# An attention kernel with a hand-written order: the third batch's fourth un-permute moved off GpSimd, a tail product kept at full width, and the order table written anew

## Chip, cores, metric

The kernel runs on one core of a Trainium2 chip. The metric is device time in microseconds (us), the median of five runs. Engines are called as the profile calls them: PE is the matrix engine (PEld its weight loads), DVE the vector engine, ACT the scalar engine, POOL the GpSimd engine, and SP the sync engine, which here only issues DMAs. A name such as SPq or POOLq is the instruction queue of that engine, where DMA issues show up.

## What is computed

Eight batches of eight-head attention over 576 positions with 64 numbers a head, with a causal mask in blocks of 64, followed by a gated feed-forward layer over all 4608 rows.

```python
scores = scale * np.matmul(q, k.transpose(0, 1, 3, 2))      # (8, 8, 576, 576)
mask = block_i >= block_j                                   # blocks of 64
attn = softmax(where(mask, scores, -1e9))
x = (attn @ v).transpose(0, 2, 1, 3).reshape(4608, 512)
out = (np.maximum(x @ w_gate, 0.0) * (x @ w_val)) @ w_out   # 512 -> 1536 -> 512
```

## The kernel before

**Tiling.** Each sequence of 576 is cut into four chunks of 128 positions and a tail of 64. A *round* r = 4*b + hp is one pair of heads hp of batch b. It makes the scores of the four chunks, transposed (keys on the partitions), takes the exponential on ACT into `attnT`, sets the masked corners to zero, and multiplies by V with a column of ones attached, so that the 65th output column is the sum that the softmax divides by. DVE divides (`normalise`, L518) into `xnat`, which is transposed into `xT`, the input of the feed-forward layer. In the first three batches the tails of all heads are done together (`tail_visit`, `last_keys`, `tail_av`); from the fourth batch on each round does its own tail.

**Feed-forward.** `ffn_gen` (L648) is a generator that emits one matrix product at each step: 96 products of the gate and the value halves and 48 of the output for each batch, 144 in all, and a ninth group for the tails of all batches. ACT takes the relu of the gate (L664), DVE multiplies it with the value product (L670), and DVE copies finished outputs out of PSUM (L749).

**The order.** Nothing is scheduled automatically. Under `manual_schedule` every engine runs its instructions in the order in which the program emits them, and each waits on semaphores for its data. The table `AT` gives every piece of work, called an act, a position: the number of feed-forward products that are emitted ahead of it. Acts are emitted in the order of their positions; acts with equal positions in the order in which the dictionary `acts` lists them; a negative position is ahead of the first product. Between 0 and 143 lie the products of the first batch, from 144 to 287 those of the second, from 288 to 431 those of the third. `HOW` says which engine or PSUM bank an act uses. So a change of position is a change of order inside the queue of each engine that the act uses, and nothing else.

**PSUM.** Three banks named `ffnp` serve the feed-forward products and many attention products in turn, `one` is a single bank, and `sc` are two double banks for the scores.

**Names that matter below:**

- `M0` to `M3`: transposes on PE of the first batch's queries and keys, pair 0 to 3, and the copies out of PSUM (L278). `p{r}{i}`: part i of the scores of round r and its exponential (L400, L414). `c{r}`: the corners. `a{r}`, `b{r}`: the products with V of the round's two heads (L576) and their division. `x{r}`: the transposes into `xT` (L619) and the copy (L620).
- `ev0`, `ev4`: POOL's casts of the second batch's V, heads 0 to 3 and 4 to 7 (L220). `tc0`: POOL's casts of the first batch's tails (L206, L207, L214). `E1v4`, `T0`: the loads that these two need, issued by SP in this order (L159, L181).
- `q2`, `q24`: for the third batch, POOL casts queries and keys of heads 0 to 3, or 4 to 7 (L195), and SP then issues two DMA transposes into the tile `perm` (L242). `u0` to `u3`: for each pair of heads, two copies (L253) that put the transposed rows in their order in `qTm` and `kTm`. `u2` and `u3` read what `q24` has transposed. `v2`: POOL's casts of the third batch's V (L228).
- `s{r}`, `e{r}`: the scores of a round from the second batch on (L450) and its exponentials (L462, L455). `S{b}`, `E{b}`, `L{b}`, `A{b}`, `B{b}`: tail scores, their exponential, the last 64 keys, and the products of tails with V for heads 0 to 3 (`A`) and 4 to 7 (`B`). `B` ends with a DMA transpose on SP (L562).
- `l3`, `lv3`: POOL issues the loads of the fourth batch (L338); `d3`: SP issues its transposes.

In the tail products, head 7 and chunk 3 has only 64 columns of weights left in its tile, so that one matrix is 64 columns wide (L545).

Of the kernel before, what the change touches and what calls it, by code (L numbers as in the profile page):

```python
# [10 lines left out]
FP = mybir.dt.float32  # L11
BF = mybir.dt.bfloat16
AX = mybir.AluOpType
# [4 lines left out]
def kernel(  # L18
# [10 lines left out]
    nc = tc.nc  # L29

    B, H, S, D = q.shape
# [4 lines left out]
    NCH = 5  # L36
# [5 lines left out]
    TW = 256  # L42

    consts = ctx.enter_context(tc.tile_pool(name="consts", bufs=1))
    sb = ctx.enter_context(tc.tile_pool(name="sb", bufs=1))
# [22 lines left out]
    attnL = [consts.tile([128, 320], BF, name=f"attnL{i}") for i in range(2)]  # L68
# [449 lines left out]
    def normalise(out, av, x=None):  # L518
        n = av.shape[1]
        rows = av.shape[0]  # L520
        recip = sb.tile([128, NCH], FP, name="recip", bufs=4)[0:rows, 0:n]
        nc.vector.reciprocal(recip, av[:, :, 64])  # L522
        m = out.shape[1]
        nc.vector.tensor_tensor(  # L524
            out=out,
            in0=av[:, 0:m, 0:64],
            in1=recip[:, 0:m].to_broadcast([rows, m, 64]),
            op=AX.mult,
        )
        if x is not None:  # L530
            nc.vector.tensor_tensor(
                out=x,
                in0=av[0:64, 4, 0:64],
                in1=recip[0:64, 4:5].to_broadcast([64, 64]),
                op=AX.mult,
            )

    def tail_av(b, g, x):

        av = psum_ffn.tile([128, 4, 65], FP, name="ffnp")  # L540
        for i in range(4):
            h = 4 * g + i
            lo = 1024 * (h % 2) + TW * (h // 2)
            for c in range(NCH):
                m = 64 if (h, c) == (7, 3) else 128  # L545
                nc.tensor.matmul(
                    av[0:m, i, :],
                    attnTt[b][:, lo + 64 * c : lo + 64 * c + m]
                    if c < 4
                    else attnL[b % 2][:, 64 * (h // 2) : 64 * (h // 2) + 128],  # L550
                    v_bf[b % 2][:, c, h, :],
                    start=(i == 0 and c == 0),
                    stop=(c == 4),
                    skip_group_check=True,
                )
        normalise(
            x[:, 256 * g : 256 * g + 256].rearrange("p (h d) -> p h d", d=64),
            av[0:64],
        )
# [5 lines left out]
    attnTt = {}  # L565
# [225 lines left out]
    dve, act, pool = nc.vector.tensor_copy, nc.scalar.copy, nc.gpsimd.tensor_copy  # L791
# [7 lines left out]
    with tc.manual_schedule(engines={E.PE, E.DVE, E.Activation, E.Pool, E.SP}):  # L799
# [25 lines left out]
        def tail_at(b):  # L825
            exps = []
            x = sb.tile([64, 512], BF, name="xtail", bufs=2)

            def begin():
                exps.extend(tail_visit(b))  # L830
                exps[0]()

            def end():
                tail_av(b, 1, x)
                tail_to_xT(b, x)

            return {
                f"S{b}": begin,
                f"L{b}": lambda: last_keys(b),
                f"E{b}": lambda: exps[1](),  # L840
                f"A{b}": lambda: tail_av(b, 0, x),
                f"B{b}": end,
            }
# [38 lines left out]
        def mains_1(hp):  # L882
# [12 lines left out]
            "v00": -59.5,  # L895
            "Lv2": -59.5,
            "Lq6": -59.5,
            "Lq4": -59.5,
            "g00": -56.5,
            "Lv4": -56.5,  # L900
            "Lv6": -54.8,
            "g01": -53.5,
            "v10": -53.5,
            "v11": -49.5,
            "v01": -49.5,
            "g10": -49.5,
            "g11": -48.91,
# [4 lines left out]
            "C1": -42.45,  # L912
            "M0": -41.16,
            "p00": -41.16,
            "j1": -41.16,
            "cq6": -40.5,
            "cq4": -40.5,
            "M1q": -37.69,
            "p02": -37.69,
            "p01": -37.69,  # L920
            "M1k": -37.69,
            "cv2": -33.09,
            "p11": -32.5,
            "cv0": -31.08,
            "M2": -29.71,
            "p10": -29.71,
            "p12": -29.71,
            "c0": -29.71,
            "c1": -20.67,
            "a0": -20.67,  # L930
            "M3": -20.67,
            "b0": -20.67,
            "p21": -20.67,
            "p20": -20.67,
# [4 lines left out]
            "b1": -17.04,  # L939
            "c2": -17.04,  # L940
            "cv4": -17.01,
            "p30": -16.5,
            "x0": -11.01,
            "x1": -10.42,
            "p32": -10.42,
            "cg00/01": -10.42,
            "a2": -10.42,
            "c3b": -7.27,
            "b2": -7.27,
            "c3a": -4.51,  # L950
            "cg00/23": -4.51,
            "cg01/23": -4.51,
            "cv6": -4.18,
            "cv00/01": -3.23,
            "v20": 3.64,
            "b3": 4.1,
# [5 lines left out]
            "g21": 7.88,  # L962
            "cv10": 8.2,
            "cv11": 8.27,
            "cg11": 8.27,
            "cv01": 8.27,
            "cg10": 8.27,
            "E1q0": 8.31,
            "v21": 8.31,
            "x3": 9.71,  # L970
            "cg20": 31.51,
# [14 lines left out]
            "cg21": 32.24,  # L986
            "cv21/0": 32.24,
            "q0": 32.24,
            "cw01": 32.3,
            "cw00": 32.32,  # L990
            "cw10": 32.32,
# [5 lines left out]
            "q4": 32.36,  # L997
            "tc0": 34.05,
            "ev4": 37.33,
            "q2": 37.71,  # L1000
            "E2q4": 37.71,
# [5 lines left out]
            "s4": 100.01,  # L1007
            "E2v0": 109.09,
            "e4": 110.34,
            "cw21/1": 110.84,  # L1010
            "c4": 112.87,
            "s5": 119.06,
            "a4": 120.37,
            "b4": 120.57,
            "e5": 120.86,
            "m2": 122.6,
            "c5": 124.25,
            "E2v4": 125.35,
            "q24": 126.26,
            "T2": 126.26,  # L1020
            "a5": 127.58,
            "s6": 128.09,
            "b5": 130.33,
            "e6": 130.65,
            "m3": 132.5,
            "c6": 133.72,
            "x5": 135.38,
            "x4": 135.4,
            "s7": 139.49,
            "a6": 139.98,  # L1030
            "b6": 141.02,
            "e7": 143.55,
            "c7": 143.96,
# [6 lines left out]
            "S0": 164.13,  # L1040
            "td1": 164.5,
            "t1": 164.55,
            "L0": 164.73,
            "E0": 169.47,
            "A0": 174.55,
            "S1": 175.78,
            "B0": 178.92,
            "L1": 179.84,
            "E1": 189.73,
            "v2": 190.06,  # L1050
            "u0": 190.06,
            "u1": 190.06,
            "s8": 198.38,
            "e8": 200.2,
            "A1": 204.6,
            "c8": 207.66,
            "u2": 207.72,
            "s9": 208.6,
            "o0": 211.5,
            "B1": 211.84,  # L1060
            "e9": 212.79,
# [3 lines left out]
            "t2": 214.73,  # L1065
            "a8": 216.59,
            "l3": 218.86,
            "lv3": 219.23,
            "u3": 222.25,
            "s10": 222.25,  # L1070
            "b8": 224.97,
            "c9": 225.44,
            "a9": 230.23,
            "b9": 230.68,
            "e10": 231.58,
            "o2": 234.34,
            "o3": 236.36,
            "x8": 237.81,
            "s11": 244.56,
            "c10": 245.9,  # L1080
            "a10": 249.57,
            "e11": 251.12,
            "b10": 253.45,
            "x9": 254,
            "x10": 255.79,
# [3 lines left out]
            "x11": 260.07,  # L1089
            "d3": 260.7,  # L1090
            "S2": 284.11,
            "L2": 291.9,
            "E2": 294.4,
            "A2": 301.64,
            "s12": 310.76,
            "L3": 315.45,
            "l4": 318.62,
            "e12": 323.23,
            "B2": 327.97,
            "c12": 332.42,  # L1100
            "lv4": 334,
            "a12": 335.18,
            "b12": 341.27,
            "s13": 345.46,
            "e13": 348.38,
            "x12": 350.72,
            "c13": 355.41,
            "d4": 356.12,
            "s14": 358.61,
# [6 lines left out]
            "b14": 381.91,  # L1116
            "x14": 384.44,
            "s15": 390.53,
            "e15": 394.34,
            "c15": 398.77,  # L1120
            "a15": 407.55,
            "b15": 407.68,
            "x15": 413.15,
# [9 lines left out]
            "u1": ("dve", "pool"),  # L1133
            "u2": ("dve", "dve"),
            "u3": ("pool", "dve"),
# [7 lines left out]
            "r11": ("dve", "sc", "ffn", None),  # L1143
# [3 lines left out]
            "r15": ("pool", "sc", "ffn", None),  # L1147
            "cv21/1": "act",
# [10 lines left out]
            "M3": ("dve", "dve"),  # L1159
# [11 lines left out]
            "cv00/23": "dve",  # L1171
        }
# [141 lines left out]
```

## Time and profile before

| what | us |
|---|---|
| median of five runs | 365.61 |
| lowest and highest of the five | 365.25, 369.18 |
| the profiled execution, its own time | 364.56 |
| its span, first to last instruction | 362.7 |
| granted PE clock over the span | 0.999 of full speed |
| ACT, exponentials of the rounds' scores, 128x1024 (L455, 56 times) | 1.044 each |
| DVE, product of gate and value, 128x512 (L670, 106 times) | 0.686 each |
| POOL, an un-permute copy (L253, 4 times) | 1.045 to 1.075 each |
| DVE, the same copy (L253, 4 times) | 0.598 to 0.959 each |
| POOL, one DMA issue of V, 128 KB or 32 KB (L338, 30 times) | 0.856 each |

The profile is of one execution; its span lies 1.9 us under its own time and 2.9 us under the median of the runs. A row of the waits reads "engine, line, waited for: total, times, longest". A row of the timeline reads "start, duration, engine, line, operation", with the idle time of the engine before it, and what ended that, in brackets. Matrix products overlap each other, so the time that one costs the engine is the distance of two starts, not the duration of one.

### The profile page before, as it was taken

What the parts mean: (1) busy time and instruction counts of PE and PEld (TensorE: products, weight loads), DVE (VectorE), ACT (ScalarE), POOL (GpSimd) and SP (SyncE); (2) the same over time, 40 slices, a digit from 0 to 9 for tenths busy, and PEclk for the clock granted to TensorE, in tenths of its full rate; (3) what the DMA queues carried; (4) which work ended last, traced back from release to release, by engine and by line L of the source; (5) the groups of instructions that cost most, each with busy time, mean ns of one, the idle gap of its engine ahead of it and who ended that gap; (6) DMA issues with size and microseconds to landing.
All of it is one profiled execution on the core that took longest, in us unless ns stands there. A gap on an engine that the chain in (4) does not pass through costs nothing.

```text
span 362.7 us, 7421 instructions
## 1 busy us (share of the span) xinstructions
PE 352.9 (97%) x2933; PEld 177.3 (49%) x2933; DVE 169.3 (47%) x422; ACT 167.4 (46%) x264; POOL 115.1 (32%) x159
## 2 busy tenths in 40 slices
PE   7799999999999999999999999999999999999996
PEld 3454454644455455545554554555455544444443
DVE  4763555567434463444444443554255434333432
ACT  4944675676236840666055625553365403302310
POOL 4647647688006800680049001930000000000000
PEclk9999999999999999999999999999999999999999
DMA  8999999999999996999449951997220130031014
GB/s 246 296 358 375 315 217 282 188 134 176 191 195 61 166 129 171 59 149 178 118 43 147 158 142 45 133 136 172 80 16 14 54 102 0 0 89 29 0 39 108
DMA packets 152083, 49.97 MB, mean 138 GB/s; under 512 B 134512, under 2 KB 145008, under 8 KB 152048
## 3 DMA queue, kind: packets, MB, share of 16 engines
q0 software_dynamic: 70480, 8.85, 45.5%
q1 hardware_dynamic: 76480, 31.86, 42.8%
q10 hardware_dynamic: 5088, 8.78, 7.5%
q8 instruction: 23, 0.38, 0.5%
q14 instruction: 12, 0.10, 0.1%
HBM read 37.75 MB, written 9.44 MB: 130 GB/s over the span
## 4 chain that ended last, share of the span: by engine, by line
PE 74%; DMA 13%; SPq 7%; POOL 4%; issue 1%; DVE 0%; POOLq 0%
PE ffnp L654 41%; PE ffnp L739 23%; DMA stage<-in_moe_w_gate_dram 4%; DMA stage<-in_k_dram 3%; DMA stage<-in_moe_w_out_dram 3%; PE sc L450 3%; SPq L159 2%; DMA k_bf<-in_k_dram 2%; PE ffnp L576 2%; PE one L450 2%; PE one L576 1%; DMA stage<-in_v_dram 1%; SPq L181 1%; SPq L169 1%; POOL q_bf L338 1%
## 5 line engine op out<-in xcount | busy, mean ns | idle before, releaser
L670 DVE TENSOR_TENSOR hT<-gate_sb,ffnp 128x512 bf16<-128x512 bf16 x106 | 72.7, 686 | 93.8 <-PE ffnp L654 69.6
L664 ACT ACTIVATE gate_sb<-ffnp 128x512 bf16<-128x512 f32 x103 | 62.1, 605 | 100.2 <-PE ffnp L654 91.3
L654 PE MATMUL ffnp<-xT,wv 128*128 128x512 bf16 x376 | 100.9, 379 | 0.0
L739 PE MATMUL ffnp<-wo,hT 128*128 128x512 bf16 (+2 forms) x444 | 99.0, 373 | 0.0
L654 PE MATMUL ffnp<-xT,wg 128*128 128x512 bf16 x364 | 98.2, 379 | 0.3 <-DVE xT L620 0.3
L739 PEld LDWEIGHTS <-hT 128*128 128x128 bf16 x444 | 41.6, 98 | 45.6 <-issue 1.1
L654 PEld LDWEIGHTS <-wg 128*128 128x128 bf16 x432 | 40.1, 98 | 44.6 <-issue 2.8
L654 PEld LDWEIGHTS <-wv 128*128 128x128 bf16 x432 | 40.0, 98 | 44.7 <-issue 2.8
L455 ACT ACTIVATE attnT<-sc 128x1024 bf16<-128x1024 f32 x56 | 56.8, 1044 | 0.0
L749 DVE COPY ob<-ffnp 128x512 f32<-128x512 f32 (+2 forms) x37 | 25.0, 676 | 44.7 <-PE ffnp L739 44.3
L338 POOL DMA_DIRECT2D q_bf<-in_q_dram x20 | 17.8, 905 | 80.1 <-DVE hT L670 55.9
L462 ACT ACTIVATE attnT<-one 128x512 bf16<-128x512 f32 (+1 forms) x28 | 15.1, 538 | 53.5 <-PE ffnp L450 53.3
L576 PEld LDWEIGHTS <-attnT 128*128 128x128 bf16 x640 | 26.6, 98 | 13.9 <-issue 1.5
L338 POOL DMA_DIRECT2D v_bf<-in_v_dram x30 | 24.3, 856 | 2.1 <-DVE xnat L524 1.0
L450 PEld LDWEIGHTS <-kTm 64*128 64x128 bf16 x384 | 11.1, 94 | 16.3 <-issue 9.6
L338 POOL DMA_DIRECT2D k_bf<-in_k_dram x20 | 17.8, 939 | 0.0
L450 PE MATMUL sc<-qTm,kTm 64*128 64x512 bf16 (+1 forms) x168 | 16.9, 305 | 0.0
L576 PE MATMUL ffnp<-v_bf,attnT 128*128 128x65 bf16 x310 | 14.5, 194 | 0.9 <-POOL v_bf L220 0.9
L462 ACT ACTIVATE attnT<-ffnp 128x512 bf16<-128x512 f32 (+1 forms) x28 | 15.0, 535 | 0.0
L522 DVE RECIPROCAL recip<-ffnp 128x5 f32<-128x5 f32 (+2 forms) x37 | 6.8, 184 | 15.4 <-PE ffnp L590 5.3
L524 DVE TENSOR_TENSOR xnat<-ffnp,recip 128x256 bf16<-128x256 f32 x31 | 13.2, 424 | 1.1
L794 DVE MEMSET attnT<- 64x128 uint32 x59 | 9.0, 165 | 9.4 <-ACT attnT L455 6.8
(120 smaller groups left out, 300.5 us busy)
## 6 DMA issues: line engine op xcount, KB each, us to landing
out_dram<-ob ACTq DMA_DIRECT2D x29, 256.0 KB, 2.3
stage<-in_moe_w_val_dram SPq DMA_DIRECT2D x6, 512.0 KB, 8.9
stage<-in_moe_w_gate_dram SPq DMA_DIRECT2D x6, 512.0 KB, 8.6
stage<-in_moe_w_out_dram SPq DMA_DIRECT2D x6, 512.0 KB, 10.5
q_bf<-in_q_dram POOLq DMA_DIRECT2D x20, 128.0 KB, 4.4
k_bf<-in_k_dram POOLq DMA_DIRECT2D x20, 128.0 KB, 5.7
v_bf<-in_v_dram POOLq DMA_DIRECT2D x20, 128.0 KB, 6.6
stage<-in_v_dram SPq DMA_DIRECT2D x19, 128.0 KB, 5.4
```

The costliest lines, as they stand in the source:

```text
L338: ins = nc.gpsimd.dma_start(dst, part_of)
L450: nc.tensor.matmul(o, kTm[b % 2][head_of(hh), c, hp, :], qT, start=True, stop=True)
L455: return lambda: nc.scalar.activation(at[:, :, lo : lo + 512], sc, AF.Exp, scale=scale)
L462: nc.scalar.activation(at[:, hh, 1024 : 1024 + w], third[hh][:, 0:w], AF.Exp, scale=scale)
L524: nc.vector.tensor_tensor(out=out, in0=av[:, 0:m, 0:64], in1=recip[:, 0:m].to_broadcast([rows, m, 64]), op=AX.mult,)
L576: nc.tensor.matmul(av[:, p, :], at[:, col : col + 128], v_bf[b % 2][:, c, h, :], start=(p == 0), stop=(c == p), skip_group_check=True,)
L654: nc.tensor.matmul(to, (wg, wv)[t][f // 4][:, c, 128 * (f % 4) : 128 * (f % 4) + 128], x[:, c], start=(c == 0), stop=(c == 3),)
L664: nc.scalar.activation(gate_sb, gate, AF.Relu)
L670: nc.vector.tensor_tensor(out=h, in0=gate_sb, in1=val, op=AX.mult)
L739: nc.tensor.matmul(op, hT[f][:, 128 * s : 128 * (s + 1)], wo[f // 4][:, f % 4, n0:n1], start=(f == 0), stop=(f == 11),)
L749: nc.vector.tensor_copy(ob, op)
L794: nc.vector.memset(o, 0.0)
```

## The change

Three things are changed.

The tail products of head 7 read their weights 64 columns further left, so that all of them are 128 columns wide. The wanted 64 rows of this head then come out in the upper half of the partitions (64 to 127) instead of the lower. The division is therefore made in up to two DVE operations: for heads 0 to 3 one, for heads 4 to 7 one on three heads and one on the last. It is written out in `tail_av` in place of the call of `normalise`.

`HOW` gives other engines to some acts: both copies of `u1` go to DVE (the keys were POOL's), `u3` goes to DVE and ACT (the queries were POOL's, the keys DVE's), the query copy of `M3` goes from DVE to ACT, one weight cast (`cv21/1`) from ACT to DVE. `cv01` is named as POOL's, where it was by default. `r11` and `r15` use other PSUM banks.

The table `AT` is replaced. Many positions differ by a few products, which leaves most queues in their old order. The diff below keeps the positions of acts that change places in a queue and are spoken of below; those of the load queue of SP change in one place at the start (`g00` ahead of `Lv4`) and in the place of `q24`.

```diff
@@ tail_av
             h = 4 * g + i
-            lo = 1024 * (h % 2) + TW * (h // 2)
+            back = 64 if h == H - 1 else 0
+            lo = 1024 * (h % 2) + TW * (h // 2) - back
+            lo_last = 64 * (h // 2) - back
             for c in range(NCH):
-                m = 64 if (h, c) == (7, 3) else 128
                 nc.tensor.matmul(
-                    av[0:m, i, :],
-                    attnTt[b][:, lo + 64 * c : lo + 64 * c + m]
+                    av[:, i, :],
+                    attnTt[b][:, lo + 64 * c : lo + 64 * c + 128]
                     if c < 4
-                    else attnL[b % 2][:, 64 * (h // 2) : 64 * (h // 2) + 128],
+                    else attnL[b % 2][:, lo_last : lo_last + 128],
                     v_bf[b % 2][:, c, h, :],
...
-        normalise(
-            x[:, 256 * g : 256 * g + 256].rearrange("p (h d) -> p h d", d=64),
-            av[0:64],
-        )
+        recip = sb.tile([128, NCH], FP, name="recip", bufs=4)
+        nc.vector.reciprocal(recip[:, 0:4], av[:, :, 64])
+        x4 = x[:, 256 * g : 256 * g + 256].rearrange("p (h d) -> p h d", d=64)
+        n = 4 if g == 0 else 3
+        for rows, i, j in ((slice(0, 64), 0, n), (slice(64, 128), n, 4)):
+            if i < j:
+                nc.vector.tensor_tensor(
+                    out=x4[:, i:j],
+                    in0=av[rows, i:j, 0:64],
+                    in1=recip[rows, i:j].to_broadcast([64, j - i, 64]),
+                    op=AX.mult,
+                )
@@ AT
...
-            "p02": -37.69,
+            "p02": -41.16,
-            "c0": -29.71,
+            "c0": -37.69,
-            "p10": -29.71,
+            "p10": -29.72,
-            "p30": -16.5,
+            "p30": -17.27,
-            "p32": -10.42,
+            "p32": -13.98,
-            "c3b": -7.27,
+            "c3b": -10.42,
-            "a2": -10.42,
+            "a2": -4.51,
-            "cv00/01": -3.23,
+            "cv00/01": 4.09,
...
-            "ev4": 37.33,
+            "ev4": 34.05,
             "tc0": 34.05,
...
-            "q24": 126.26,
+            "q24": 191.07,
             "T2": 126.26,
-            "B0": 178.92,
+            "B0": 178.89,
             "u0": 190.06,
             "u1": 190.06,
-            "v2": 190.06,
+            "v2": 191.07,
             "u2": 207.72,
-            "A1": 204.6,
+            "A1": 210.5,
-            "B1": 211.84,
+            "B1": 220.2,
-            "s10": 222.25,
+            "s10": 221.68,
             "u3": 222.25,
-            "l3": 218.86,
+            "l3": 217.2,
-            "lv3": 219.23,
+            "lv3": 223.89,
...
-            "s15": 390.53,
+            "s15": 383.65,
-            "e15": 394.34,
+            "e15": 383.74,
@@ HOW
-            "u1": ("dve", "pool"),
+            "u1": ("dve", "dve"),
             "u2": ("dve", "dve"),
-            "u3": ("pool", "dve"),
+            "u3": ("dve", "act"),
...
-            "r11": ("dve", "sc", "ffn", None),
+            "r11": ("dve", "one", "ffn", None),
...
-            "r15": ("pool", "sc", "ffn", None),
-            "cv21/1": "act",
+            "r15": ("pool", "ffn", "ffn", None),
+            "cv21/1": "dve",
...
-            "M3": ("dve", "dve"),
+            "M3": ("act", "dve"),
...
+            "cv01": "pool",
```

## Prediction

> **What bounds the kernel now.** I read the totals first, then PE's waits by stretch, then the timeline around each wait.
>
> ```profile
> PE 352.9 (97%) x2933; PEld 177.3 (49%) x2933; DVE 169.3 (47%) x422; ACT 167.4 (46%) x264; POOL 115.1 (32%) x159
> ```
>
> PE is busy for all but 9.8 us of the span, no other engine for half of it. Since matmuls overlap, busy is not yet full rate; but in the chain of waits 96 products take 20.72 us, 0.216 each, and I find no slower stretch of such products after the start. So the span shrinks only where PE waits or where its own work shrinks. The view of PE's waits, asked for 22 to 60 us and for 60 us to the end, answers with one row each:
>
> ```profile
> PE ffnp L576 <- POOL v_bf L220: 0.9, 1, 0.9
> ...
> PE one L450 <- POOL qTm L253: 0.9, 1, 0.9
> ```
>
> All other listed waits of PE lie before 22 us, and 3.5 us after the last product (the final copy and store) stay as they are. The timeline shows what stands behind the two.
>
> ```profile
> 49.94 0.62 POOL L195 CAST k_bf<-stage 128x512 bf16<-128x512 f32 x1 [0.20 <-DMA stage<-in_k_dram]
> ...
> 53.80 0.61 POOL L206 CAST q_bt<-stage 64x512 bf16<-64x512 f32 x1 [3.24 <-DMA stage<-in_q_dram]
> ...
> 55.61 1.06 POOL L220 CAST v_bf<-stage 128x1024 bf16<-128x1024 f32 x1
> ...
> 56.72 0.46 PE L576 MATMUL ffnp<-v_bf,attnT 128*128 128x65 bf16 x10 [0.85 <-POOL v_bf L220]
> ...
> 84.55 3.53 POOL L338 DMA_DIRECT2D v_bf<-in_v_dram  x4
> ...
> 89.08 1.32 POOL L338 DMA_DIRECT2D v_bf<-in_v_dram  x2 [0.99 <-DVE xnat L524]
> ...
> 90.44 1.04 POOL L253 COPY qTm<-perm 128x512 bf16<-128x512 bf16 x1
> ...
> 91.54 0.27 PE L450 MATMUL one<-qTm,kTm 64*128 64x256 bf16 x1 [0.87 <-POOL qTm L253]
> ```
>
> In the first group POOL stands 3.24 us for the tails (`tc0`) while `ev4`, which PE needs, is queued behind. In the second `u3`'s query copy is behind all of POOL's DMA issues for the fourth batch; PE waits 0.87 us for it.
>
> **The change, part by part.** Sums are made against the profiled execution (span 362.7, own time 364.56); the median of the runs, 365.61, is 1.05 above that time, and I carry savings over to the median.
>
> *`ev4` ahead of `tc0`: -0.85.* Its loads were issued on SP's queue between 45.27 and 48.48, ahead of the tail query load (48.58) that landed by 53.80. With the 5.3 us median to landing of such loads they are there by 53 to 53.8; the cast (1.06) ends at 54.1 to 54.9. PE wants it at 56.72 - 0.85 = 55.87. The tail casts move back by some 1 us at most, and `q2` behind them starts as before (same total on POOL). Bounds: 0 if the load lands after 54.8, else 0.85. I take 0.85: the row of the next load says 53.80.
>
> *`u3` to DVE and ACT: -0.87.* POOL loses 1.05. DVE's part changes from the keys (0.60) to the queries (0.66 to 0.67, `u2`'s and `u1`'s rows); ACT gets a copy of 0.60 to 0.64 (L278's rows). Both sit near 83 us, where ACT is busy 1.35 of 2 us and DVE 1.90; `s11`, which needs them, is 22 products (4.8 us) behind. `u1`'s keys likewise add 0.60 to 0.96 to DVE at 72 to 74 us, where it is busy 1.27 of 2. Priced at nothing; cover gone, 0.6 each.
>
> *No 64-column matmul: -0.7.* In `B0` the last head starts at 70.50 and the next work at 70.87, 0.37; the head before takes 68.36 to 68.50 in the like place of `A0`, 0.14. In `B1` 80.68 to 81.06, in `B2` 114.17 to 114.55. Three times 0.23. DVE pays one more operation on 64x64 for each (0.206) and saves a quarter of 0.417, +0.1 each, behind which only the tail's DMA transpose waits.
>
> *`q24` behind `B0` and `v2`: +0.3, the doubtful term.* Before, its casts ended at 64.4 and its transposes were issued at 70.18 and 73.37; `u2` on DVE at 79.21 waited for nothing. Now POOL must run `u0`, wait for `B0`'s products (70.8 before, about 70.0 with the savings ahead of it), run `v2` (2.03) and then the two casts (2.1): about 74.1. On SP the transposes are now behind `B0`'s own transpose (1.2 us of issue, its input ready at 71.7) and go out at about 73.2 and 74.4. They landed 5.3 and 3.4 us after issue; that gives 78.5 and 77.8, while DVE reaches `u2` at about 79.21 - 0.85 - 0.2 = 78.2. Queued behind `u2` on DVE are the products L670 and the divisions, for which PE's banks wait. The sharper question is what shares the DMA engines. POOL's issues for the fourth batch started at 75.21; they now start some 0.5 later (two casts more, a load wait of 0.78 and the 0.85 less). The row of the transposes issued at 83 to 87 us, in the middle of those loads, says 6.8 to 8.7 us. The Trainium skill (DMA: Bandwidth & Descriptors, "Issuing engines are not separate DMA queues") says that DMAs of all issuing engines end up on the same 16 DMA engines and interleave. By the row of 5.3 the wait is 0.3 or less; taking the rule for the whole transfer, 8.7 us, they land at 81.9 and 83.1, and `u2` ends at 84.1 instead of 80: 4 us late, of which PE forgives about 1.0 (a gate and value pair takes it 1.72, DVE needs 0.69 of that for the bank), so +2.9. The transposes are half through when the loads start, so I am nearer the first: +0.3, with 0 and +2.9 as ends.
>
> A second rule speaks against giving DVE these copies: by the skill (GPSIMD Engine Reference, Key points) POOL shares its memory interfaces with DVE and contends with two-port DVE instructions. The rows: `u2`'s key copy took 0.96 at 79.81, `u3`'s 0.60 at 83.82, both beside POOL's DMA issues, and POOL's four issues took 3.60 across the first against 3.67 with none. By the rule three copies at 0.96; by the better row 0.60 to 0.67. One us of DVE between them, not of PE, so the sum stays, except that the 0.3 above would become 0.6.
>
> *The start: 0.* ACT's queue sets it: twelve exponentials from 6.83 to 17.79, with an idle 0.49 at 10.33.
>
> ```profile
> 10.38 0.50 PE L400 MATMUL sc<-qTm,kTm 64*128 64x512 bf16 x4
> ...
> 10.81 5.99 ACT L414 ACTIVATE attnT<-sc 128x1024 bf16<-128x1024 f32 x7 [0.49 <-PE sc L400]
> ...
> 16.70 0.58 ACT L620 COPY xT<-ffnp 128x512 bf16<-128x512 bf16 x1
> ...
> 17.17 0.62 ACT L414 ACTIVATE attnT<-sc 128x512 bf16<-128x512 f32 x1
> ...
> 17.65 0.41 DVE L620 COPY xT<-ffnp 128x512 bf16<-128x512 bf16 x1
> ...
> 18.12 0.81 PE L654 MATMUL ffnp<-xT,wg 128*128 128x512 bf16 x3 [0.29 <-DVE xT L620]
> ```
>
> `p10` no longer waits behind `M2`'s transposes, which wait for POOL's casts: the 0.49 goes. `M3`'s copy (0.60) comes in. `p32` goes ahead of `x0`: it ends about 0.5 earlier, `x0`'s copy 0.5 later, near 17.8. The first feed-forward product waits for that, but the next three waited for `x1` until 18.12 anyway, and `x1` on DVE stays at 17.5 to 18, now behind `c3b`. Then DVE carries `a2`, `b2`, a cast, `b3`, `a3` at 0.55 or 0.42 each to about 20.5, as before (20.45), and the twelfth product comes at 21.6. What is late next is DVE. Bounds: -1.5 (its 0.69 less for `M3` and ACT's 0.5 both count) to +0.7 (`x0` late by its whole copy). Middle: 0.
>
> *The rest: 0.* `s15` and `e15` go to the first product of an output group, where ACT has no relu for 48 products (10 us); other moves are of a few products, and no wait of PE is listed there that they could take away.
>
> Sum: -0.85 - 0.87 - 0.7 + 0.3 = -2.1. Span 360.6, profiled time 362.4, median 363.5.
>
> **The rivals.**
>
> *The start gains too.* For it: ACT's and PE's small waits before 18.2 us (0.69, 0.32, 0.50, 0.22, 0.29) hang on one another. With -1.5 there and no loss at `u2`: -3.9, median 361.7. Against it: DVE's five operations, above.
>
> *Slower: `u2` holds DVE.* If the transposes take 8.7 us, -2.4 + 2.9 = +0.5, median 366.1; each further us of landing costs one more, as PE then has no bank. It decides from a landing 8.2 us after issue, and over 1% slower needs 12. For it: rows of 8.0 (`q2`'s, behind loads) and 8.7. Against it: `q24`'s own 5.3 and 3.4.
>
> *The waits only move.* PE arrives 0.85 earlier at 57 us and meets the next late thing, say the exponentials of round 7 or the tail loads; then only the 0.7 and perhaps one wait remain: -1.0, median 364.6. Against it: no other wait is listed after 22 us, and DVE and ACT follow PE in that stretch.
>
> **How the numbers follow.** The sum as worked out 0.45, waits that move 0.17, the start gains too 0.27, `u2` holds DVE 0.11. About 1% (3.7 us) is what a measurement of this kernel can tell from no change; the body cannot give more than 2.4, so "faster by over 1%" is the start's case and takes its 0.27, a little generously. Slower by over 1% takes 0.11, stretched for stalls that I do not see; within 1% has 0.62. The range goes from 360.8 (start at its best, -2.4 - 1.5 and 0.9 of spread between runs: four of the five lie within 1.0) to 366.8 (the slow case, half a us worse than its price).
>
> **What would show it.** No wait of PE on L220 near 56 us and none on L253 near 91 us; the last head of `B` at 0.14; DVE's copies L253 near 78 us with an idle of 0.5 or less before them that ends with the DMA `perm`; the twelfth product at 21.6. Wrong: an idle of over 2 us on DVE at `u2` with PE waiting, a first product after 18.3 with the twelfth after 22.2, or a new wait row of PE after 22 us.

## The result and the profile after

The changed kernel takes 363.0 us (median of 43 runs, 39 of them between 362.3 and 365.7) against 366.0 for the kernel before beside it (78 runs): a ratio of 0.993, 95% interval 0.9917 to 0.9944. The ratio leaves out three runs of the changed kernel that took 410, 522 and 611 us at a granted clock of 0.57 to 0.85. Its profiled execution took 364.26 us over a span of 362.5, at a granted clock of 0.999.

First the totals on the page of the changed kernel.

```profile
PE 353.0 (97%) x2933; PEld 176.9 (49%) x2933; DVE 170.3 (47%) x426; ACT 167.8 (46%) x265; POOL 113.3 (31%) x157
```

Its view of PE's waits lists none from 22 to 60 us, and from 60 us to the end this one:

```profile
PE ffnp L663 <- DMA xT<-xnat: 1.0, 1, 1.0
```

Both waits of before are gone, and a wait of 1.0 us for a DMA transpose is new. The timeline of the changed kernel at the places that the forecast named:

```profile
53.60 1.06 POOL L220 CAST v_bf<-stage 128x1024 bf16<-128x1024 f32 x1 [2.99 <-DMA stage<-in_v_dram]
54.61 0.61 POOL L206 CAST q_bt<-stage 64x512 bf16<-64x512 f32 x1
...
56.20 0.47 PE L585 MATMUL ffnp<-v_bf,attnT 128*128 128x65 bf16 x10
...
69.41 0.29 PE L547 MATMUL ffnp<-v_bf,stage 128*128 128x65 bf16 x4
69.53 0.20 PE L547 MATMUL ffnp<-v_bf,attnL 128*128 128x65 bf16 x1
...
78.00 0.60 DVE L253 COPY qTm<-perm 128x512 bf16<-128x512 bf16 x1
...
83.70 0.76 DVE L253 COPY qTm<-perm 128x512 bf16<-128x512 bf16 x1
...
89.68 0.28 PE L450 MATMUL one<-qTm,kTm 64*128 64x256 bf16 x1
...
103.47 0.79 PE L663 MATMUL ffnp<-xT,wg 128*128 128x512 bf16 x2 [1.00 <-DMA xT<-xnat]
```

`ev4` stands ahead of the tails and PE passes at 56.20 without a wait; `B0`'s last head is as short as the others (the one before it starts at 69.26); `u2` on DVE begins without idle; `u3` is done long before round 11 at 89.68. At 103.47 PE is early, and what it wants is not there.

To see where time is won and lost, I follow one landmark through all kernels: the start of DVE's product of gate and value (L670, or L679 in the kernels with the new `tail_av`). The table gives its distance to the kernel before, in us, for the profiled execution of each kernel: the first product of the first feed-forward batch, the first and the eleventh of the second, the first of the third and of the fourth. From there to the last such product nothing changes by more than 0.02. The last two columns are the median of all runs and the ratio to before with its interval. The experiments ran in three groups, each beside its own runs of before (medians 367.4, 366.5 and 366.6), so ratios are compared between groups, and medians only inside one.

| kernel | 1st | 2nd batch | its 11th | 3rd | 4th | median | ratio |
|---|---|---|---|---|---|---|---|
| changed | +0.52 | -0.47 | -1.26 | -0.48 | -0.34 | 363.0 | 0.993 (0.992 to 0.994) |
| changed, again | +0.54 | -0.45 | -1.23 | -1.82 | -0.81 | 363.02 | 0.991 (0.988 to 0.994) |
| narrow product back | +1.30 | +0.32 | +0.18 | -0.40 | -0.36 | 363.42 | 0.991 (0.989 to 0.993) |
| `ev4` behind tails | +0.53 | -0.46 | -0.97 | -1.55 | -1.73 | 363.65 | 0.993 (0.990 to 0.995) |
| start of before | -0.04 | -1.02 | -1.80 | -2.38 | -1.22 | 362.58 | 0.990 (0.987 to 0.994) |
| three parts alone | +0.03 | -0.99 | -0.46 | -1.38 | -1.29 | 363.55 | 0.995 (0.992 to 0.997) |
| `u3` on POOL behind loads | +0.80 | -0.19 | -0.95 | +5.82 | +5.64 | 367.13 | 1.001 (0.998 to 1.005) |
| `u3` on POOL ahead of loads | +0.50 | -0.48 | -1.27 | -1.85 | -2.04 | 362.66 | 0.992 (0.989 to 0.995) |
| start of before, `ev4` behind | +0.77 | -0.21 | -0.94 | -1.53 | -1.71 | 363.48 | 0.990 (0.985 to 0.995) |
| before, loads behind pair | +0.65 | +0.91 | +1.49 | +0.55 | +0.56 | 363.99 | 0.992 (0.989 to 0.995) |
| start of before, `u3` ahead | -0.06 | -1.04 | -1.81 | -2.18 | -0.46 | 363.48 | 0.989 (0.984 to 0.994) |
| weight cast behind `x2` | +0.42 | -0.56 | -1.35 | -1.54 | +0.15 | 362.4 | 0.988 (0.983 to 0.993) |

The two kinds of column do not say the same. By its profile the changed kernel gains 0.3 us, by its runs 2.6 (the ratio) to 3.0 (the medians); "before, loads behind pair" loses 0.56 in its profile and gains 2.6 in its runs. The profile of before is the main reason: it took 364.56 us, and of the 82 runs of before in the experiments only two were as quick. The profiles of these two kernels, for their part, lie 1.3 and 1.1 us above the medians of their runs.

### The profile page after: what moved, and what is told of

Same layout as the page of the kernel before. It is cut to its first block, busy times and chain, and to the rows that moved or that the text cites. A ratio compares the mean times of both kernels' runs of the same rounds, so it can differ in the third digit from the quotient of the medians.

```text
span 362.5 us, 7423 instructions
## 1 busy us (share of the span) xinstructions
PE 353.0 (97%) x2933; PEld 176.9 (49%) x2933; DVE 170.3 (47%) x426; ACT 167.8 (46%) x265; POOL 113.3 (31%) x157
## 4 chain that ended last, share of the span: by engine, by line
PE 88%; DMA 5%; ACT 4%; DVE 1%; issue 0%; POOL 0%; POOLq 0%; DVEq 0%
PE ffnp L663 49%; PE ffnp L748 23%; PE sc L450 3%; DMA xT<-xnat 3%; PE one L450 2%; PE ffnp L585 2%; DMA stage<-in_moe_w_gate_dram 2%; PE one L585 2%; ACT attnT L414 2%; PE one L663 1%; ACT attnT L455 1%; PE ffnp L547 1%; PE one L794 1%; PE ffnp L599 1%; PE one L599 1%; DMA qTt<-q_bt 1%
## 5 line engine op out<-in xcount | busy, mean ns | idle before, releaser
L679 DVE TENSOR_TENSOR hT<-gate_sb,ffnp 128x512 bf16<-128x512 bf16 x106 | 72.7, 685 | 96.0 <-PE ffnp L663 67.6
L450 PEld LDWEIGHTS <-kTm 64*128 64x128 bf16 x384 | 11.1, 94 | 15.1 <-issue 7.7
L585 PE MATMUL one<-v_bf,attnT 128*128 128x65 bf16 x250 | 11.7, 193 | 0.7 <-POOL v_bf L220 0.7
## 6 DMA issues: line engine op xcount, KB each, us to landing
stage<-in_moe_w_out_dram SPq DMA_DIRECT2D x6, 512.0 KB, 10.6
```

The source lines that it names most:

```text
L450: nc.tensor.matmul(o, kTm[b % 2][head_of(hh), c, hp, :], qT, start=True, stop=True)
L585: nc.tensor.matmul(av[:, p, :], at[:, col : col + 128], v_bf[b % 2][:, c, h, :], start=(p == 0), stop=(c == p), skip_group_check=True,)
L679: nc.vector.tensor_tensor(out=h, in0=gate_sb, in1=val, op=AX.mult)
```

## The experiments

**The changed kernel again.** No edit.

> The changed kernel once more, for a second profile. My account of the changed profile: +0.5 us at the start, about -2.5 us from the three parts, and a wait of 1.0 us of PE for a DMA transpose of xT at 103 us that belongs to one execution and not to the kernel. Theory (the wait comes and goes): ratio to before 0.993, and a profile that may well lack the 1.0 us wait, its span then near 361. Rival (the wait is a fixed price of the new order): the same wait of PE for xT near 103 us again, about 1 us, and a span of 362.5.

The start is late again (+0.54), but for another reason than in the first profile. There ACT's cast of a gate weight waited 2.48 us for its load, with the copy of `x2` queued behind it (both rows stand under the last experiment). Here the cast waits 0.36, and the copy behind it 1.31 for PE, whose clock was at half from 8.8 to 12.2 us:

```profile
18.32 0.62 ACT L382 CAST wg<-stage 128x512 bf16<-128x512 f32 x1 [0.36 <-DMA stage<-in_moe_w_gate_dram]
20.25 0.58 ACT L629 COPY xT<-one 128x512 bf16<-128x512 bf16 x1 [1.31 <-PE one L628]
```

The 1.0 us wait for `xT` is not there, so it belongs to the execution and not to the kernel, but the view of PE's waits lists another in its place:

```profile
PE one L472 <- DMA kTt<-k_bt: 0.8, 1, 0.8
```

**The narrow product back.** `tail_av` as before, with its 64-column product; all else as changed.

> The changed kernel with the old tail products (64 columns for head 7, chunk 3). Theory: the narrow product costs PE 0.23 us in each of three places, so +0.7 us against the changed kernel in the same call, ratio to before about 0.995, and the last head of B takes 0.37 instead of 0.14 in the profile. Rival (it is hidden behind other waits): no difference, below 0.2 us.

The timeline of this kernel in `B0`:

```profile
70.04 0.28 PE L546 MATMUL ffnp<-v_bf,stage 128*128 128x65 bf16 x4
70.16 0.20 PE L546 MATMUL ffnp<-v_bf,attnL 128*128 128x65 bf16 x1
70.19 0.40 PE L546 MATMUL ffnp<-v_bf,stage 128*128 128x65 bf16 x4
70.53 0.20 PE L546 MATMUL ffnp<-v_bf,attnL 128*128 128x65 bf16 x1
```

From the first product of the last head to its fifth it takes 0.34 (70.19 to 70.53), against 0.12 for the head before. In the changed kernel both take 0.12, so a place costs 0.22. Against the changed kernel this execution is 0.78 behind at the start (its clock, too, was at half from 8.8 to 12.3 us), 1.44 after two places (0.2 more than these make), and nearly level (0.08) at the third feed-forward batch, where the changed kernel waited for DMA and this one didn't. In the runs its median is 0.4 above that of the changed kernel, with intervals that overlap.

**`u3` on POOL, first try.** `u3` on POOL and DVE, `lv3` at 219.23 as before. That puts the fourth batch's V loads ahead of the tail products of the second batch's heads 4 to 7 (`B1`, now at 220.2), which then read the fourth batch's V. So a position can decide what is read, and not only when; this part of the computation is changed.

> The changed kernel with the query copy of u3 on POOL again, behind the issue of the fourth batch's V loads (lv3 at its old position), the key copy on DVE. Theory: PE waits at round 11 for this copy as it did before, 0.9 us or more, since PE is now 1.5 us earlier there while POOL's issues end no earlier: +0.9 to +2.4 us against the changed kernel. Rival (something else would be late at the same place, so the wait had only been the last of several): +0.3 or less.

377.34 us, ratio 1.029 (1.025 to 1.033). PE waited 11.1 us in those products for the loads and never in round 11, so the run says nothing on `u3`; two kernels further down separate the copy from the loads.

**`ev4` behind the tails.**

```diff
-            "ev4": 34.05,
+            "ev4": 37.33,
```

> The changed kernel with POOL's cast of the second batch's V, heads 4 to 7, behind the tail casts again. Theory: PE's wait for it near 56 us is back, +0.85 us at most, less the +0.5 by which PE is later there now: +0.3 to +0.85 against the changed kernel, and a wait row of PE on L220 near 56 us. Rival (the waits only move): +0.1 or less.

Timeline of this kernel:

```profile
53.33 0.61 POOL L206 CAST q_bt<-stage 64x512 bf16<-64x512 f32 x1 [2.83 <-DMA stage<-in_q_dram]
...
54.82 1.06 POOL L220 CAST v_bf<-stage 128x1024 bf16<-128x1024 f32 x1
...
56.21 0.47 PE L585 MATMUL ffnp<-v_bf,attnT 128*128 128x65 bf16 x10
```

The cast ends at 55.88, PE comes at 56.21, since its start was 0.5 us late: no wait in either order, and -0.46 here against -0.47. In the runs, 0.993 against 0.991, the intervals overlap.

**The start of before.** All positions below 10 and the engine of `M3` as before.

> The changed kernel with the order of its start put back: every entry of the order with a position below 10 has the number it had before, and the third mask copy is again on DVE. Theory (the new start costs 0.5 us, since ACT's weight cast waits for a later load and the copy of the third x block is queued behind it): the 12th product of the first FFN batch starts at about 21.6 us in place of 22.1, the products of the second batch are 1.0 us or more ahead of those of before, and the end is up to 0.5 us earlier than that of the unchanged changed kernel: 362.4 to 363.0. Rival (what is saved ahead of 97 us is given back between 97 and 112 us, where the fourth batch's DMA transposes set the pace): the start is 0.5 us earlier, and the end is where it was, 363.0 to 363.7.

The first product is back at before's place and the second batch 0.55 further ahead than in the changed kernel. Past 97 us PE waits for DMA transposes (this kernel's timeline):

```profile
106.70 1.21 SPq L117 DMA_TRANSPOSE kTt<-k_bt  x1
...
110.02 0.29 PE L472 MATMUL one<-qTt,kTt 128*128 128x64 bf16 x4 [0.79 <-DMA kTt<-k_bt]
```

The last of them is issued at 106.70, hardly other than in before (106.49), although PE is 2.4 us earlier; the gain at the third batch, 2.38, is 1.22 at the fourth. The median of six runs is lower than the changed kernel's by an amount that the intervals don't separate.

**The three parts alone.** The kernel before with three edits:

```diff
+ tail_av as changed
-            "ev4": 37.33,
+            "ev4": 34.04,
-            "u3": ("pool", "dve"),
+            "u3": ("dve", "act"),
```

> The kernel before with three parts of the change alone: the tail products with the last head in the lower rows, the third batch's fourth pair on DVE and ACT, and the fifth piece of batch 1's V cast ahead of the tail casts. Nothing else of the order is moved, and the start is the old one. Theory (the three terms of the forecast, 0.85 + 0.87 + 0.7, are the whole gain, and the rest of the new order adds the 0.5 at the start and nothing else): the second FFN batch starts 0.8 to 1.0 us ahead of before, round 11 (by 92 us) 2.2 to 2.4 us ahead, the end 2.4 us ahead, or less by what the stretch from 97 to 112 us gives back; ratio to before 0.993 to 0.996. Rival (the rest of the order carries a good part of it): under 1 us of gain, ratio over 0.997.

Timeline of this kernel:

```profile
55.83 0.47 PE L585 MATMUL ffnp<-v_bf,attnT 128*128 128x65 bf16 x10
...
81.42 0.76 DVE L214 CAST v_bf<-stage 64x256 bf16<-64x256 f32 x1
...
83.51 0.28 PE L450 MATMUL one<-qTm,kTm 64*128 64x256 bf16 x1 [0.48 <-DVE xnat L524]
```

With the start on time, `ev4`'s move is worth what the forecast said: PE at 55.83 without a wait against 56.72, and 0.99 in hand at the second batch. Half of it goes at 83 us, where a cast on DVE beside POOL's DMA issues took 0.76 in place of 0.29 and the tail's added division 0.17 more (0.59 for its two operations, 0.42 for the one of before), so that the division behind them came late. The ratio, 0.9945, is in the theory's range; its interval (0.9917 to 0.9974) just touches the rival's.

**`u3` on POOL behind the loads, and ahead of them.** Two kernels, the changed one with `"u3": ("pool", "dve")`; in the first also:

```diff
             "lv3": 223.89,
-            "u3": 222.25,
+            "u3": 223.9,
```

> The changed kernel with the third batch's fourth pair un-permuted by POOL (q) and DVE (k) again, and in POOL's order behind the fourth batch's V loads, as it was before. Theory (the pair was late because POOL issues those loads first): POOL copies q after about 91 us (after 95 us if the loads are held up as in the profile of the changed kernel), round 11 needs it at 89.7 us, so TensorE waits 2 to 6 us there in front of the score products and the end is 1 to 5 us later than that of the changed kernel (a part may be made up for, since the stretch from 97 to 112 us has slack for TensorE). Rival (the wait only takes the place of the one for the DMA transposes): the end moves by less than 0.4 us.

> The changed kernel with the third batch's fourth pair on POOL (q) and DVE (k), but in POOL's order ahead of the fourth batch's V loads, in the place where the changed kernel has the pair. Theory (the place in POOL's queue counts, not the engine): POOL copies q at about 86 us in 1.0 us, 2.5 us before round 11 needs it, TensorE doesn't wait, and the time is that of the changed kernel within 0.3 us. Rival (the copy is slow on POOL or arrives late for itself): a wait for POOL at about 89.7 us and a time over 364.

The timeline of the first kernel, with the pair behind the loads:

```profile
93.68 0.62 POOL L338 DMA_DIRECT2D v_bf<-in_v_dram  x1 [0.94 <-DMA out_dram<-ob]
94.34 1.04 POOL L253 COPY qTm<-perm 128x512 bf16<-128x512 bf16 x1
...
95.44 0.37 PE L450 MATMUL one<-qTm,kTm 64*128 64x256 bf16 x1 [5.38 <-POOL qTm L253]
```

The same kernel by stretches of 1 us (stretch, length, busy time and number of instructions of PE, PEld, DVE, ACT and POOL, PE's granted clock, DMA share, GB/s):

```profile
91.00:92.00 1.00, 0.00 (x0) 0.00 (x0) 0.00 (x0) 0.00 (x0) 0.34 (x1) 1.00 1.42 271
92.00:93.00 1.00, 0.00 (x0) 0.00 (x0) 0.00 (x0) 0.00 (x0) 0.63 (x1) 0.82 2.17 161
93.00:94.00 1.00, 0.00 (x0) 0.00 (x0) 0.00 (x0) 0.00 (x0) 0.32 (x1) 0.50 2.81 151
...
98.00:99.00 1.00, 1.00 (x13) 0.72 (x12) 0.30 (x2) 0.33 (x1) 0.00 (x0) 0.50 2.10 91
99.00:100.00 1.00, 1.00 (x11) 0.44 (x9) 0.30 (x1) 0.00 (x0) 0.00 (x0) 0.76 0.04 1
```

The loads were held up, the copy came at 94.34, and PE stood for 5.38 us. What held them up is not shown: the rows name a store of the output (0.94), a load of `k_bf` (0.77) and a matrix product (0.91), in before a division (0.99). Its clock fell to half at about 92.6 (0.82 is the mean of that us) and was back at about 99.5, so that 4 us of work ran at half speed, which costs 2 more. The third batch starts 7.67 later than in the second kernel, 0.3 of which was there before. That one copies ahead of the loads (its timeline), and has no listed wait from 60 us to the end:

```profile
84.55 1.08 POOL L253 COPY qTm<-perm 128x512 bf16<-128x512 bf16 x1
85.57 2.65 POOL L338 DMA_DIRECT2D v_bf<-in_v_dram  x3
```

In the runs, 367.13 against 362.66: with the pair behind the loads the whole gain of the change is gone; with the pair on POOL, but ahead of them, all of it is there, as far as the intervals tell. So it is the place in POOL's queue that counts; the choice of engine makes no difference that these runs can show.

**Before, with the loads behind the pair.** One number of the kernel before:

```diff
-            "lv3": 219.23,
+            "lv3": 222.3,
```

> The kernel before with one number of the order changed: the fourth batch's V loads are issued behind the un-permuting of the third batch's fourth pair (222.3 in place of 219.23), and the pair stays on POOL and DVE. Theory (the 0.9 us for which TensorE waited for POOL's copy was the loads ahead of it in POOL's queue): the wait is gone, round 11 comes 0.9 us earlier against the products ahead of it, the end 0.5 to 0.9 us earlier, ratio to before 0.9975 to 0.9985. Rival 1 (the loads come too late for the fourth batch, or the stretch from 97 to 112 us takes the gain): no change, 1.000. Rival 2 (the pair waits for something else next): a wait for DVE or for DMA in round 11, under 0.4 us of gain.

The ratio is 0.992 (0.989 to 0.995): 2.6 us between the medians, three times the most that the theory allowed, and about as much as the whole change. PE doesn't wait for POOL's copy any more, as its timeline shows. What its profiled execution lost, it lost elsewhere: a start at half clock (see the next experiment), 1.2 us of wait for `ev4` (0.85 in before), and 0.5 for a division at 85 us.

```profile
85.30 1.54 POOL L253 COPY qTm<-perm 128x512 bf16<-128x512 bf16 x1
86.78 3.53 POOL L338 DMA_DIRECT2D v_bf<-in_v_dram  x4
...
92.10 0.28 PE L450 MATMUL one<-qTm,kTm 64*128 64x256 bf16 x1
```

The profiled execution was the slowest of its twelve runs (365.12; the others 363.26 to 364.57). The twelve lie within 1.9 us, the 17 runs of before beside them within 9.1.

**The start of before and `ev4` behind the tails.**

> The changed kernel with the start of before, and on top of it the fifth piece of batch 1's V cast behind the tail casts in POOL's order, as it was before. Theory (the cast's move was worth 0.85 us, and was worth nothing in the other experiment only because TensorE came there half a us later): TensorE waits again at about 55.7 us for that cast, 0.3 to 0.9 us, and the second FFN batch starts that much later than in the kernel with the start of before alone (62.6 to 63.2 us in place of 62.30); end later by as much or by less. Rival (the cast is early enough in either place): no wait there, the second FFN batch at 62.3 us.

No wait at `ev4`, but the test fell through: in this execution the start was late too, by 0.77, for another reason. The stretch from 9 to 13 us in this kernel, and the same row of the kernel before (columns as above):

```profile
9.00:13.00 4.00, 3.55 (x25) 2.02 (x27) 2.54 (x6) 2.57 (x4) 3.48 (x8) 0.57 1.20 290
```

```profile
9.00:13.00 4.00, 3.14 (x37) 1.68 (x34) 2.88 (x6) 3.51 (x5) 3.47 (x7) 1.00 1.20 291
```

The cast ended at 55.91 and PE came at 56.45; with the start on time it comes at 55.64 (as in the kernel with the start of before alone), which would make a wait of 0.3. That is worked out, not seen.

**The start of before and `u3` ahead on POOL.**

> The changed kernel with the start of before, and with the third batch's fourth pair on POOL (q) and DVE (k) ahead of the V loads. Theory (the two gains add, since one is at the start and the other leaves POOL's queue without a held-up load): the second FFN batch at 62.3 us, the end 0.5 us ahead of the kernel with the pair on POOL ahead of the loads alone, span about 360.1, median 362.0 to 362.5, ratio to before 0.988 to 0.991. Rival (the stretch from 97 to 112 us takes it): 362.6, as either of the two alone.

The gains add up to the third batch (-2.18) and are spent behind it: waits of 0.5 for `kTm` and 1.0 for `kTt`. The rival held. The median of its six runs, 363.48, is no better than that of either alone.

**ACT's weight cast behind `x2`.**

```diff
-            "cg01/23": -3.47,
+            "cg01/23": 4.2,
```

> The changed kernel with one number of the order of its start changed: the cast of a quarter of the second gate weight that ACT does stands behind the copy of the third x block in ACT's order (4.2 in place of -3.47), so that the copy doesn't wait for the weight's load. Theory (this cast alone made the start 0.5 us late): ACT copies the block at about 19.7 us in place of 20.35, the 12th product of the first FFN batch starts at 21.5 to 21.8 us in place of 22.1, and the second FFN batch 0.3 to 0.5 us earlier. Rival (the products that need this quarter now wait for it, or another load or DVE's masks hold the start): the 12th product at 22.1 us or later.

Timelines of the changed kernel, then of this one:

```profile
17.42 0.39 PE L663 MATMUL ffnp<-xT,wg 128*128 128x512 bf16 x1
...
19.83 0.62 ACT L382 CAST wg<-stage 128x512 bf16<-128x512 f32 x1 [2.48 <-DMA stage<-in_moe_w_gate_dram]
20.35 0.58 ACT L629 COPY xT<-one 128x512 bf16<-128x512 bf16 x1
...
20.98 0.38 PE L663 MATMUL ffnp<-xT,wg 128*128 128x512 bf16 x1 [0.28 <-ACT xT L629]
```

```profile
17.75 0.39 PE L663 MATMUL ffnp<-xT,wg 128*128 128x512 bf16 x1
...
20.13 0.58 ACT L629 COPY xT<-one 128x512 bf16<-128x512 bf16 x1 [2.56 <-PE one L628]
20.61 0.62 ACT L382 CAST wg<-stage 128x512 bf16<-128x512 f32 x1
```

The product that the forecast calls the twelfth (by the records of before and of the changed kernel it is the thirteenth) came at 22.00, between the two expectations. But this execution was 0.33 later already at its first product; counted from there, the twelfth is 4.25 behind in this kernel, 4.68 in the changed one, 4.12 in before. So the cast cost 0.43 of the 0.56. A version that beats the changed kernel for certain wasn't found: this one and the two others with medians of 362.4 to 362.7 have intervals that contain it.

## Why the prediction was right, and where it was not

The time was forecast at 363.5 and came at 363.0, but the terms that make it up were not the ones that carry it. That the sum came out is in part luck: `ev4` and the narrow product were counted in full and little of them was kept, and `u3` was counted at a third of what it gave. (The upper end of the range, half a us above the slow case's 366.1, should have been 366.6 and not 366.8; nothing hangs on it.)

*`u3`, -0.87: right in mechanism, too small.* It is most of the gain. Undoing it alone brings the kernel back to 1.001, and one moved number in the kernel before, which has only this effect, gives 0.992. The price was read from one execution, and that one was among the quickest: its last V load was issued by 90.4. In the twelve other profiles (without the first try on POOL), all of them of other kernels, it was between 91.2 and 94.9, in three of them with the copy ahead of it. In before the copy stands behind it, and PE is there at 90.7, so a us of hold-up in POOL's queue would be a us of PE's. In the wait of 5.38 us the clock fell too. 26 of the 82 runs of before have a mean clock of 0.992 or less, with a median of 368.6 against 366.2 for the rest; of 103 runs of the kernels of the table without the pair behind the loads, the changed kernel's first runs aside, three have one. How long the wait is in an ordinary run of before, and how often the clock falls in it, is inferred from this; only one execution of it was profiled. The Trainium skill (TensorE: Matmul & The Clock Gate, Part 1) puts the fall to half rate behind at least one idle window of about 3.4 us, which runs free of the kernel. In the wait of 5.38 us it came sooner, 2.6 us after the last product's end; in the 8.3 us wait of the first try on POOL it came 5.0 us after. Half rate lasted 6.8 us in the one and 10.2 in the other, two and three times the 3.4 us for which it lasted at the start of five executions. So the rows bear out the length of the window, and one of the two cases not the whole idle window that the page asks for.

*`ev4`, -0.85: shown where the start is on time, and worth nothing in the changed kernel's own profile.* The kernels with the old start have 0.99 to 1.04 in hand at the second batch. In the changed kernel PE arrives 0.5 late, and the cast would have been in time in its old place.

*The narrow product, -0.7: right in each place* (0.22 to 0.23 at `B0`, `B1` and, by 113.86 to 114.01 against 114.17 to 114.55, at `B2`), but the first two lie ahead of the stretch that gives time back. 0.4 was left between the medians of the runs, which the intervals do not tell from nothing.

*`u2`, +0.3: zero, and the working had a mistake in it.* `q24` and `v2` have the same position, and the list of acts puts `q24` first, so its casts ran at 68.34 and 69.32, not at 72 to 74. That did not bring the transposes forward: SP was busy with loads and with `B0`'s own transpose, and issued them at 73.45 and 74.80, as forecast, by another road. They landed in 3.3 and 3.2 us, and DVE came at 78.00 and didn't wait. That they landed sooner because POOL's loads began only at 75.90 is not shown: the transpose of before that took 5.3 us, issued at 70.18, was nearly through when the loads there began at 75.21. The rival "`u2` holds DVE" fell.

*The start, 0: wrong by +0.5, inside its bounds.* The forecast looked to DVE; it was ACT, whose cast of a weight waited 2.48 for its load with `x2`'s copy queued behind. No step of the working asked what ACT's moved cast waits for. The new start has this wait, of 2.3 to 2.6, in the four profiles with the cast in this place that had the full clock from 9 to 13 us; in the three that had half of it the load was there 1.3 to 1.8 us sooner, the cast waited 0.4 to 0.5, and the start was late (0.54 to 1.30) with PE. Why the load lands sooner there is not known.

*The rival "the waits only move": half true.* It named round 7 or the tail loads, and it happened at 97 to 112 us, where SP's DMA transposes for the third batch's input and the fourth batch's keys land at nearly the same time whenever PE gets there: `kTt`'s transpose was issued between 105.9 and 108.4 in all profiles but that of the 5.38 us wait and of the first try on POOL. By the fourth batch up to 1.7 us were given back there, in some executions and not in others. That the rest of the new order brings nothing is not excluded by the three parts alone (0.995 against 0.991 to 0.993, overlapping), nor is it shown to bring anything.

## What to carry to other kernels

Before costing a wait from one profile, ask how far that execution lies from the median of its kernel; a wait that ends behind a queue of DMA issues is a sample of something that varies, and its mean can lie well above what the trace shows (here, by inference, at three times). Then look at the place in the queue before the engine: moving the loads behind the copy, one number, was worth about as much as giving the copy to other engines. And for each piece moved forward in a queue, look up what it waits for, since everything behind it inherits that wait.

## What the runs showed of the hardware

- A wait of 5.38 us of PE cost it over 7: the granted clock fell to half 2.6 us after its last product and came back 4 us after work resumed. In a wait of 8.3 us (first try on POOL) it fell 5.0 us after the last product and came back 7.0 after the next one.
- Five of the twelve experiments, with the old start and the new, had a mean clock of 0.57 to 0.60 between 9 and 13 us in their profile, the others 1.00: 3.4 us at half rate. With the old start the two that had it were 0.65 and 0.77 us late, the three that had not within 0.06. With the new start the three that had it were 0.54 to 1.30 late, the five that had not 0.42 to 0.80.
- DVE's cast of 64x256 numbers at 80 to 84 us took 0.29 us in four of the profiles and 0.76 to 0.84 in the other ten, beside POOL's DMA issues in each; what decides between the two was not looked into.
- POOL took 5.9 us to issue the six V loads in before, and up to 7.7 elsewhere (three parts alone, 84.10 to 91.83). Beside them the fourth batch's loads landed in 4.3 to 9.5 us in before, in 5.9 to 10.6 in the changed kernel (medians by tensor).
